# Retention scores by row halves, states by head with one scan, one mask table: a fused retention and Fourier-mixing kernel on one core

## The chip, the cores and the metric

The kernel runs on one core of a Trainium2 chip. The metric is the device time of one execution in microseconds (us). The kernel before takes 236.49 us, the median of three runs (236.26 to 236.76). The profile of before is one more execution, of 236.86 us.

The engines of a core work side by side, each through its own queue in program order: TensorE (PE in the profile; its weight loads are PEld), VectorE (DVE), ScalarE (ACT), GpSimd (POOL) and SyncE (SP), which issues transfers. Engines wait for each other by semaphores. TensorE writes only into PSUM, which has eight banks here used as a few shared slots; VectorE and ScalarE empty them.

## The reference

Inputs are q, k, v of shape (4 batches, 8 heads, 768 tokens, 64) and two weight matrices (512 x 2048 and 2048 x 512).

1. Retention: for each head a 64 x 64 state is carried along the tokens, `state = gamma[h] * state + k_t v_t^T` with `gamma[h] = 1 - 2^(-5-h)`, and `y_t = q_t state / 8`. The heads side by side give x of shape (4, 768, 512).
2. Fourier mixing: `u = x + real(FFT over tokens and features of x)`.
3. Layer norm of u without weights, then `out = u + relu(un @ w_ch1) @ w_ch2`.

## The kernel before

**Retention in chunks.** Tokens go in 6 chunks of 128 (`NCH = 6`). Heads go in four pairs per batch (`PAIR_ORDER`), 64 + 64 = 128 partitions. For each pair and chunk there are three products:

- *Scores* inside the chunk, keys by queries, masked and weighted by the decay: `a_piece` (line 691) on TensorE, `ma_piece` (705) on VectorE.
- *Key-value products* of chunks 0 to 4, 64 x 64 for each head, from which the *states* at the chunk borders come by a decayed running sum: `kv_piece` (717) and `s_piece` (731).
- *Output*: scores by v (`y_piece`, 753) plus queries by the state of the chunk before (`yx_piece`, 744), gathered in PSUM (`wkY`), then scaled into x by `x_piece`, mostly on ScalarE.

**Batch 0 and the later batches differ.** Batch 0 has units of its own:

- `am_unit` (line 574) takes the scores of a head as a product over 64 partitions only, head 0 in the upper and head 1 in the lower half of the rows, each into its own PSUM bank. `ae_unit` (583) multiplies by one 128 x 128 table `maskf` and the head's constant at the same time.
- `kv0_unit` (598) takes the 64 x 64 product of each head alone, head 0 into PSUM partitions 0 to 63 and head 1 into 64 to 127, with the five chunks as the innermost index: element (e, c) lies at `5*e + c`.
- `sc_unit` (607) makes all five states of a pair by one `tensor_tensor_scan` over 320 values, with the decay table `gk5` (zero at c = 0, so that each column begins anew).
- `yx_unit` (630) reads `s16[sl, :, c - 1]`, again by halves of the rows.

Batches 1 to 3 use full 128-row products instead. `qTz` holds the queries of each head with zeros in the other head's 64 rows, so that one product of the pair's keys with 2 x 128 columns of `qTz` gives both heads' scores: six products of 256 columns a pair, in three pieces of two chunks, one PSUM bank a piece. `ma_piece` multiplies 512 values a partition with `maskp`, a table with a mask for every head, which eight units `mp0` to `mp7` fill on various engines early on. `kv_piece` takes the full 128 x 128 product of the pair, of which only the two diagonal blocks are used, in two banks (chunks 0 to 2, and 3 and 4). `s_piece` copies the first state and makes the other four by a `scalar_tensor_tensor` each, on VectorE, into `s16[P, 5, 128]`. `yx_piece` reads 64 neighbouring values of it.

**The rest of a batch.** The Fourier mixing is done with cosine and sine tables after folding tokens and features by symmetry (`fold_s`, `fold_d`, `fold_e`, `s1_piece` at 840, `s2_piece` at 1024, `u_piece`). Then come layer norm, a first layer (`h3_piece`, 1267; relu in `r3_piece`, 1276), and a second layer by a seven-product scheme on half blocks (`hs_piece`, `m_piece` at 1329, `p3_piece` at 1374). The scheme needs sums of weights, `wsum_unit`; one of them, `ws1`, is laid over the memory of `gk5`, which is no longer used after batch 0.

**What sets the order.** `ORDER` is a written list of some 1,450 units for the whole kernel, and `pin()` chains every engine's instructions in just that order. `ENGINES` gives, unit by unit, the engine of a copy or scaling (A ScalarE, D VectorE, P GpSimd). Units are named by batch, kind, part and pair: `2a0_1` is the first score piece of batch 2, pair 1. `f512` is a filler, a 512-column product on dummy data, used in batch 0's stretch. Waits follow from tiles: the pool `ps_g` has 5 PSUM slots shared by scores, key-value products, `wkY`, transposes and the Fourier products; `ps_pm` has 3 for the two layers. Loads of batches 2 and 3 wait for the last score product of pair 1 of the batch before (`a_of`).

Of the kernel before, what the change touches and what calls it, by code (L numbers as in the profile page):

```python
# [36 lines left out]
q0:A q1:P q2:A q3:P k00:D k10:P k20:P k30:A v00:P v10:P v20:P v30:P v31:P eq0:D eq1:D eq2:A  # L37
eq3:A ek00:A ek10:A ek20:A ek30:A x00:A x01:D x10:A x11:D x20:A x21:A x30:A x31:A tn0:D tn1:A
tn2:D tn3:D tn4:A gk0:P gk1:A gk2:P gk3:A gc00a:D gc01a:D gc01b:D gc10a:A gc11a:A gc11b:A
ste0:A ste1:A xn0:P xn1:P cdh0:A cdh1:P nsp:P hid5:A fs0a:D fs0b:D fla:D flb:D fha:D fhb:D  # L40
fd0:D fd1:D gr0:D gr1:A gr2:A gr3:P nid0:D nid1:A hid:P v01:P eb0:D v11:P eb1:D v21:P eb2:A
eb3:A mp6:A mp5:A qn1:A mp1:P qn2:A un1:D h00:A te1:D mp2:P xl2:P qn3:A xl3:P mp0:D qn0:D h02:A
h12:A qn4:A h13:A xu2:D h03:A un2:A h11:A h01:A te2:A xl4:P xu4:P xu3:P xl0:D un3:A xu0:D h10:A
h20:D un4:A h21:A qn5:D xl5:P 1ck1_0:P te3:A h22:A 1cq_0:D 1ck0_0:D 1ek_0:D 1eq0_0:A 1eq1_0:A
xu5:P 1cv_0:P 1s0_0:A un5:A 1cq_1:A te4:D 1ck0_2:A 1ck0_1:P 1ck1_1:P mp7:P 1eq1_1:A 1eq0_1:A
1cv_1:P 1ek_1:A 1x1_0:A mp3:P 1x0_0:A h23:A 1cv_2:P 1ck1_2:A 1s0_1:D te5:A 1cq_3:P 1cq_2:A
1ck0_3:P 1s0_2:D 1cv_3:P 1ek_2:A mp4:P 1eq1_2:A 1ck1_3:P 1eq0_2:A 0r1_12:A 1eq1_3:A 1eq0_3:A
1x1_1:A 1x0_1:A 1s0_3:A 0r1_5:A 1ek_3:A 0r1_7:A 0r1_8:A 1x0_2:A 1x1_2:A 2cv_1:A 2cq1_1:A
# [12 lines left out]
1r2_4:A 1r2_3:A 2q1_2:A 1r2_5:A 2q0_2:A 1r2_2:A 3x1_1:A 1r2_7:A 3cq1_3:P 2q1_4:D 3cv_2:A
3x0_1:A 2q0_4:D 3cq1_2:D 3cq0_2:A 3ck0_2:P 2q0_5:A 2q1_5:A 2ux1_3:P 3x0_0:A 2ux1_4:P 3s0_3:A
2ux1_2:P 2ux0_3:P 2r0_1:A 3s0_2:A 2ux0_2:P 2ux0_4:P 2r0_2:A 2r0_5:A 2r0_7:A 2ux1_5:P 2r0_3:A
2r0_4:A 2r0_0:A 2ux0_5:D 2r0_6:A 3x1_0:A 3x0_2:A 3x1_2:D 3x1_3:A 2r1_5:A 2r1_6:A 3x0_3:A
2r1_1:A 2r1_3:A 2r1_2:A 2r1_4:A 2r1_0:A 2r1_7:A 3g00:A 3g11:A 3gr11:A 3g01:A 3g10:A 3q1_1:A
3gr10:A 3q0_1:D 3q0_0:D 3q1_0:A 3q1_2:D 3q0_2:D 3ux0_0:P 2r2_6:A 3ux1_0:P 2r2_2:A 2r2_7:A
3ux0_1:P 3ux1_2:P 2r2_0:A 3ux1_1:P 3gr00:P 2r2_1:A 3ux0_2:P 2r2_3:A 2r2_5:A 2r2_4:A 3gr01:D
3q1_3:A 3q0_3:D 3ux0_3:P 3q0_5:A 3ux1_3:P 3r0_3:A 3q0_4:A 3q1_5:D 3r0_6:A 3r0_7:A 3r0_4:A
3r0_5:D 3r0_1:A 3r0_0:D 3q1_4:D 3r0_2:A 3ux1_5:P 3ux0_5:P 3ux0_4:P 3r1_1:A 3ux1_4:P 3r1_5:A
3r1_4:A 3r1_0:D 3r1_2:A 3r1_6:D 3r1_3:A 3r1_7:D 3r2_2:D 3r2_3:A 3r2_6:A 3r2_4:A 3r2_1:A 3r2_0:A  # L70
3r2_7:D 3r2_5:A
# [3 lines left out]
lq0 nid0 lk0 par gk3 f512 q0 lv0 qtz10 lq1 ta0 v00 ta1 tn1 f512 f512 f512 f512 tb1 si1 k00 tk0 qz0  # L75
q1 mp2 lk1 lv1 lq2 qtz00 lk2 ab1 tq0 lq3 tn0 gk2 eq0 tb0 ta2 tn2 f512 ek00 am01 ab0 ae010 nid1 kb0
k10 co1 tb2 si2 hid5 ab2 co2 ae011 tq1 am00 ae001 si0 f512 f512 eb0 ta3 tk1 ek10 lk3 f512 tn3 eq1
tb3 lv2 ab3 v01 kv0 ae000 yi01 kb1 gk0 v11 sc0 si3 q2 mp6 f512 v10 f512 k20 gk1 nsp yi00 co0 eb1
am11 ae110 ae111 am10 ae101 ae100 tk2 ek20 tq2 yx0 eq2 x01 kv1 q3 f512 x00 f512 f512 w10 w11 sc1
am21 ae210 ae211 am20 mp3 ae201 yi10 k30 ae200 kb2 eb2 yi11 yx1 x11 f512 x10 fs0a fs0b tk3 ta4 tq3  # L80
v20 ek30 v21 kv2 sc2 tn4 tb4 w12 kb3 eq3 am30 yi20 ae301 mp7 ae300 ab4 am31 hid ae311 si4 eb3 yi21
yx2 ae310 stx01 lv3 v30 v31 kv3 s1s10 w13 w20 sc3 x20 x21 flb yi31 yi30 co4 fla fd1 yx3 f512 s1s00
x30 fd0 s1m1 x31 fha fhb co3 cdh0 xn0 g0a s1m0 xm0 gc00a s1s01 gc01a gc10a xmb xn1 s1s11 gc11b
gc11a w21 g0b g0c gc01b stx3 stg00 stx4 stg01 cdh1 xm2 stg10 stg11 stx2 ste1 half qe1 s22 qn2 gr0
ste0 close px1 s21 qn1 uu1 xm1 ul1 gr3 gr1 gr2 mu1 un1 h00 h03 ul2 w22 s20 xl2 uu2 qn0 s23 qn3 xu2
s25 xe qz1 ul3 qtz01 ut1 uu0 te1 xl3 ul0 h01 w23 h02 mu2 0p0_0 un2 bn2 mp0 xl0 s24 qn4 uu4 ul4 xl4
uu3 qn5 ul5 xl5 xu3 h11 pad11 ut2 te2 h13 1lq0 1lk0 h10 1lq1 xu0 bn0 1lk1 h22 bn1 bn3 xu4 1lv0 h20
h21 0rt0 bn4 0p1_0 uu5 0p2_0 un3 h12 1cq_1 0p3_0 xu5 0p0_2 1cq_0 1tq0 1tq1 1ck1_0 1ck1_1 1ck0_0
1tk0 1lq2 un4 ut4 bn5 0p1_2 1ek_0 1eq0_0 0rc0 mp1 0o0 0p0_1 1ck0_1 te4 1tk1 1eq1_0 1a2_0 qtz11
1a0_0 1m0_0 un5 1eq0_1 1eq1_1 1cq_2 1lk2 1cv_0 1m2_0 1ek_1 1lv1 1cv_1 pad01 1lk3 1ck0_3 1lq3 1cq_3  # L90
1kv0_0 1s0_0 0p1_1 1s1_0 ut3 te3 0p2_1 1a1_0 1kv1_0 1m1_0 1a0_1 1m0_1 1ck0_2 1a2_1 1s2_0 0p3_1
1s3_0 1s4_0 1lv3 1m2_1 1a1_1 1ck1_2 1tk2 1ek_2 ut5 te5 1m1_1 h23 1tq2 1kv0_1 1s0_1 1ck1_3 1cv_3
1yx_0 1y1_0 mp5 1y0_0 1eq0_2 1eq1_2 1s1_1 1s2_1 1kv1_1 1x1_0 1lv2 1cv_2 0o1 1x0_0 2lq1 2lk1 0p2_2
0p3_2 1s3_1 1a1_2 1s4_1 1m1_2 1tk3 1ek_3 1a0_2 1m0_2 1tq3 1kv0_3 0h1_8 1s0_3 1s1_3 0o2 0r1_8 1yx_1
1y1_1 1y0_1 1eq0_3 1s2_3 pad10 1kv0_2 1s0_2 2lv1 1s1_2 0h1_6 1eq1_3 1x0_1 2lk0 1x1_1 1s2_2 1a2_2
0h1_12 2cq1_1 1kv1_2 1m2_2 1a0_3 0r1_6 2lk2 0r1_12 mp4 1s3_2 0h1_11 0r1_11 1s4_2 1m0_3 1a2_3 1m2_3
1yx_2 1kv1_3 1y0_2 1s3_3 1y1_2 1a1_3 1m1_3 1s4_3 0rt1 1x1_2 1x0_2 1fs00 1fs01 0h1_1 1fd01 0r1_1
# [71 lines left out]
def kernel(  # L169
# [518 lines left out]
    def a_piece(b, i, part):  # L688
        def run():
# [6 lines left out]
            if part == 2:  # L696
                a_of[b, i] = mm
# [931 lines left out]
```

## Time and profile before

| what | value |
|---|---|
| median of three runs | 236.49 us (236.26 to 236.76) |
| the profiled execution | 236.86 us |
| its span in the trace | 234.9 us |
| TensorE busy | 228.9 us |
| VectorE busy | 203.4 us |
| ScalarE busy | 144.3 us |
| GpSimd busy | 91.3 us |
| granted TensorE clock | 1.00 |

The span runs from the first to the last instruction of the program. A group is written as line, engine, operation, output <- inputs, form, count. For a matmul the form begins with rows*columns of the array in use: 128*128 is the whole of it, 64*128 half of the rows, 128*64 half of the columns. The length of a matmul includes the way through the array, in which the next has already begun; the pace is told by the distance from start to start.

### The profile page before, as it was taken

The page shows a single profiled execution, that of the slowest core. Times are in us where ns is not written, and L with a number is a line of the kernel's source. Part 1 is how long each engine was busy: PE and PEld are TensorE (multiplying, and loading weights), DVE is VectorE, ACT ScalarE, POOL GpSimd, SP SyncE. Part 2 cuts the span into 40 slices and gives each one's busy share as a digit, 9 for nine tenths or more (in the row PEclk, how much of TensorE's full clock was granted, in tenths as well). Part 3 has the DMA queues.
Part 4 walks back from the last instruction along what each step waited for, and adds up shares of the span by engine and source line. Part 5 has one row for each costly group of instructions (what it writes and reads, how often), then busy time and mean ns, then how long its engine had stood idle before and what let it go on. Part 6 is the DMA issues. An engine that isn't in the chain of part 4 may idle for free.

```text
span 234.9 us, 6332 instructions
## 1 busy us (share of the span) xinstructions
PE 228.9 (97%) x2471; PEld 187.1 (80%) x2471; DVE 203.4 (87%) x527; ACT 144.3 (61%) x303; POOL 91.3 (39%) x144
## 2 busy tenths in 40 slices
PE   7999999999999999999999999999999999999994
PEld 2566888856776855889999989888898988888884
DVE  6599989966899999999999999999988698875494
ACT  7599786688998856671976493565644615241220
POOL 4789133452440378226315707404007161330302
PEclk9999999999999999999999999999999999999999
DMA  7999997999999999999969956632700224130034
GB/s 199 311 290 178 207 166 116 257 228 247 220 213 201 211 209 176 198 195 182 237 161 202 201 129 126 156 77 81 237 3 4 45 89 114 22 47 0 4 125 143
DMA packets 94253, 36.45 MB, mean 155 GB/s; under 512 B 83600, under 2 KB 91408, under 8 KB 94224
## 3 DMA queue, kind: packets, MB, share of 16 engines
q1 hardware_dynamic: 89856, 31.79, 63.9%
q0 software_dynamic: 4224, 4.19, 11.5%
q8 instruction: 19, 0.31, 0.6%
q14 instruction: 10, 0.08, 0.1%
q10 hardware_dynamic: 144, 0.07, 0.1%
HBM read 27.26 MB, written 6.29 MB: 143 GB/s over the span
## 4 chain that ended last, share of the span: by engine, by line
PE 73%; ACT 1%; DVE 0%; issue 0%
PE psh L1267 27%; PE psc L1329 24%; PE psc L1223 6%; PE psh L1183 4%; PE wkA L694 3%; PE ps L840 3%; PE pq L1024 2%; PE wkY L753 2%; PE wkY L744 1%; PE wkK L717 1%; ACT qTz L262 1%; PE tq L669 1%; PE psh L1205 0%; PE pst L1167 0%; PE ps L974 0%; ACT x L267 0%
## 5 line engine op out<-in xcount | busy, mean ns | idle before, releaser
L1267 PE MATMUL psh<-unT,w 128*128 128x256 f16 x576 | 67.7, 273 | 0.0
L1267 PEld LDWEIGHTS <-w 128*128 128x128 f16 x576 | 55.8, 98 | 6.6 <-DVE u L1374 0.2
L1276 ACT ACTIVATE ht<-psh 128x512 f16<-128x512 f32 x65 | 37.4, 596 | 30.5 <-PE psh L1267 22.7
L1329 PEld LDWEIGHTS <-ht 128*128 128x128 f16 x360 | 34.1, 98 | 4.2 <-DVE ht L1300 0.3
L1329 PE MATMUL psc<-w,ht 128*128 128x256 f16 x192 | 26.2, 272 | 0.0
L705 DVE TENSOR_TENSOR atm<-wkA,maskp 128x512 f16<-128x512 f32 x36 | 23.9, 682 | 1.5 <-PE wkA L694 1.5
L1060 POOL TENSOR_TENSOR u<-u,x 128x256 f32<-128x256 f32 x31 | 19.7, 654 | 14.2 <-DVE u L1050 7.9
L1223 PE MATMUL psc<-w,ht 128*128 128x512 f16 x96 | 23.3, 379 | 0.0
L1374 DVE TENSOR_TENSOR u<-psc,u 128x256 f32<-128x256 f32 x42 | 16.7, 416 | 6.6 <-PE psc L1329 5.8
L1374 POOL TENSOR_TENSOR u<-u,cd 128x512 f32<-128x512 f32 (+1 forms) x8 | 8.9, 1119 | 27.9 <-DVE cd L1374 27.9
L267 ACT ACTIVATE x<-wkY,gexp 128x384 f16<-128x384 f32 x29 | 16.1, 583 | 5.6 <-PE wkY L753 4.1
L731 DVE SCALAR_TENSOR_TENSOR s<-s,gk,wkK 128x128 f16<-128x128 f16 x48 | 16.1, 341 | 2.2 <-ACT s L262 1.5
L1118 DVE BATCH_NORM_STATS2 bst<-u 128x6 f32<-128x512 f32 x24 | 16.3, 681 | 0.2
L263 POOL COPY g16r<-g 128x384 f16<-128x384 f16 x6 | 3.4, 579 | 31.5 <-ACT g L262 19.0
L1223 PEld LDWEIGHTS <-ht 128*128 128x128 f16 x96 | 8.7, 98 | 7.7
L262 ACT COPY qn<-pq 128x127 f32<-128x127 f32 (+2 forms) x31 | 7.9, 299 | 11.0 <-PE pq L1024 5.1
L1374 POOL TENSOR_TENSOR u<-u,ws 128x256 f32<-128x256 f32 (+1 forms) x6 | 5.7, 978 | 20.5 <-DVE ws L1374 20.5
L1399 ACT ACTIVATE un<-u,stats 128x512 f16<-128x512 f32 x12 | 9.5, 812 | 5.8 <-DVE stats L1392 5.8
L694 PE MATMUL wkA<-qTz,kT 128*128 128x256 f16 x72 | 12.4, 272 | 0.3 <-ACT unT L262 0.2
L268 POOL TENSOR_SCALAR kd<-k,gexp 128x384 f16<-128x384 f32 x15 | 9.4, 629 | 6.8 <-DMA k<-in_k_dram 4.8
L1183 PE MATMUL psh<-unT,w 128*128 128x384 f16 x64 | 11.9, 326 | 0.0
L1205 PE MATMUL psh<-unT,w 128*128 128x128 f16 x192 | 11.7, 219 | 0.0
(238 smaller groups left out, 508.5 us busy)
## 6 DMA issues: line engine op xcount, KB each, us to landing
q<-in_q_dram SPq DMA_DIRECT2D x16, 384.0 KB, 6.2
k<-in_k_dram SPq DMA_DIRECT2D x16, 384.0 KB, 5.6
v<-in_v_dram SPq DMA_DIRECT2D x16, 384.0 KB, 6.3
w<-in_moe_w_ch_dram POOLq DMA_DIRECT2D x8, 512.0 KB, 7.8
out_dram<-u SPq DMA_DIRECT2D x6, 512.0 KB, 3.4
out_dram<-u SPq DMA_DIRECT2D x6, 256.0 KB, 3.9
out_dram<-o SPq DMA_DIRECT2D x2, 512.0 KB, 3.2
out_dram<-o SPq DMA_DIRECT2D x3, 128.0 KB, 1.8
```

The source lines that it names most:

```text
L267: return nc.scalar.activation(out, in_, AF.Copy, bias=0.0, scale=scale)
L694: mm = nc.tensor.matmul(wk[:, c2], st["kT"][:, c, :], st["qT"][:, :, c, :], start=True, stop=True)
L705: nc.vector.tensor_tensor(out=st["atm"][:, 2 * part:2 * part + 2], in0=st["wk", part], in1=maskp[:, PAIR_ORDER[i]].unsqueeze(1).to_broadca ...
L731: nc.vector.scalar_tensor_tensor(out=s16[:, c], in0=s16[:, c - 1], scalar=gk2[:, hp:hp + 1], in1=st["kv", c // 3][:, c % 3], op0=ALU.mult, ...
L1060: (nc.vector if on.get(f"{b}ux{n}_{kb}", "P") == "D" else nc.gpsimd).tensor_tensor(out=u[:, lo:hi], in0=u[:, lo:hi], in1=x[:, 1, 257:1:-1] ...
L1118: nc.vector.bn_stats(bst, lb[b]["u"][:, kb, :])
L1183: nc.tensor.matmul(psh, w116[:, cb, fb * P:(fb + 1) * P], lb[b]["unT"][:, cb, rt * 384:(rt + 1) * 384], start=(cb == 0), stop=(cb == 3))
L1223: nc.tensor.matmul(lb[b]["psc", rb], ht16[:, fb, rb % 3 * P:rb % 3 * P + P], w216[:, fb, :], start=(fb == 0), stop=(fb == NFB - 1))
L1267: nc.tensor.matmul(psh[:, t], w116[:, cb, fb * P:(fb + 1) * P], lb[b]["unT"][:, cb, p * 256:(p + 1) * 256], start=(cb == 0), stop=(cb == 3))
L1276: nc.scalar.activation(dst, psh, AF.Relu, bias=0.0, scale=1.0)
L1329: nc.tensor.matmul(o if c1 - c0 == 256 else o[:, c0:c1], lh(f), r, start=first and f == 0, stop=last and f == 7, skip_group_check=True)
L1374: (nc.vector if e == "D" else nc.gpsimd).tensor_tensor(out=o, in0=x, in1=y, op=ALU.add)
```

## The change

Batches 1 to 3 take batch 0's forms for three steps of the retention, and the written order and the engines of the units are new throughout:

- *Scores*: twelve products over 64 rows instead of six over 128, in two pieces of three chunks; each piece fills two banks, one a head. The mask step becomes four operations of 3 x 128 values a pair, with the one table `maskf` and the head's constant. `maskp` and its eight units go.
- *Key-value products and states*: `kv0_unit` and `sc_unit` now serve all batches, one bank and one scan a pair. `kv_piece` and `s_piece` go.
- *State products*: `yx_piece` stays at full height with `qTz`, but reads the state as `s16[:, :, c - 1]`, whose 64 values lie 5 apart.
- `ws1` becomes a tile of its own, since `gk5` is needed to the end.
- `ORDER` has 1,381 units instead of 1,450, with one `f512` less; many units of `ENGINES` change place or engine.

```diff
-    maskp = const.tile([P, NHP, 2, P], f32, tag="maskp")
+    ws1 = const.tile([P, 8, 256], f16, tag="ws1")
...
-    def kv0_unit(i):
+    def kv0_unit(i, b=0):
         def run():
-            st = st_of(0, i)
-            kd, v16 = kd_of[0, i], v16_of[0, i]
+            st = st_of(b, i)
+            kd, v16 = kd_of[b, i], v16_of[b, i]
...
-    def sc_unit(i):
+    def sc_unit(i, b=0):
...
     def a_piece(b, i, part):
         def run():
             st = st_of(b, i)
-            wk = st["wk", part] = ps_g.tile([P, 2, 2, P], f32, tag="g", name="wkA")
-            for c2 in range(2):
-                c = 2 * part + c2
-                mm = nc.tensor.matmul(wk[:, c2], st["kT"][:, c, :], st["qT"][:, :, c, :],
-                                      start=True, stop=True)
-            if part == 2:
+            wk = st["wk", part] = [ps_g.tile([P, 3, P], f32, tag="g", name="wkA",
+                                             padded_shape=[P, 4, P]) for _ in range(2)]
+            for c3 in range(3):
+                c = 3 * part + c3
+                for h2 in range(2):
+                    sl = slice(D * h2, D * h2 + D)
+                    mm = nc.tensor.matmul(wk[h2][:, c3, :], st["kT"][sl, c, :],
+                                          st["qT"][sl, h2, c, :], start=True, stop=True)
+            if part == 1:
                 a_of[b, i] = mm
...
-    def ma_piece(b, i, part):
+    def ma_piece(b, i, part, h2):
...
-            nc.vector.tensor_tensor(
-                out=st["atm"][:, 2 * part:2 * part + 2], in0=st["wk", part],
-                in1=maskp[:, PAIR_ORDER[i]].unsqueeze(1).to_broadcast([P, 2, 2, P]),
-                op=ALU.mult)
+            nc.vector.scalar_tensor_tensor(
+                out=st["atm"][:, 3 * part:3 * part + 3, h2, :], in0=st["wk", part][h2],
+                scalar=float(gam[2 * PAIR_ORDER[i] + h2] ** (-P)),
+                in1=maskf.unsqueeze(1).to_broadcast([P, 3, P]), op0=ALU.mult, op1=ALU.mult)
...
-    def kv_piece(b, i, g):
...
-    def s_piece(b, i, c):
...
                     nc.tensor.matmul(yk[h2][:, c, :], st["qT"][:, h2, c, :],
-                                     st["s16"][:, c - 1, 64 * h2:64 * h2 + 64],
+                                     st["s16"][:, :, c - 1],
                                      start=(c == 1), stop=False, skip_group_check=True)
...
-    ws1 = gk5.rearrange("p h e c -> p (h e c)").bitcast(f16)[:, 0:2048].rearrange(
-        "p (f m) -> p f m", m=256)
```

More of the change, by code (lines that the diff above doesn't have):

```diff
@@ L36 @@
 ENGINES = """
[L37 to L48, printed above, removed]
@@ L67 @@
[L67 to L71, printed above, removed]
+q0:A q1:P q2:A q3:D k00:D k10:P k20:P k30:P v00:P v10:A v20:P v30:P v31:P eq0:D eq1:D eq2:A
+eq3:A ek00:D ek10:A ek20:A ek30:A x00:A x01:A x10:A x11:A x20:A x21:A x30:A x31:A tn0:A tn1:A
@@ new lines @@
+2cq0_0:A 1q1_2:A 2ck0_3:P 1q0_2:A 1gr11:A 1gr10:D 1q1_3:A 1q0_3:A 2cv_0:P 1ux0_1:P 1q0_5:A
+1ux1_0:P 1ux0_0:P 2ck0_2:P 1q1_5:A 1ux1_1:D 2ck1_2:A 1ux0_2:P 1q1_4:A 1ux0_3:P 2ck1_3:P
+1ux1_3:P 1ux1_2:P 2cq0_2:A 2cq1_2:A 1ux0_5:P 2cq0_3:P 2x1_1:A 1te0:A 1q0_4:A 1te1:A 2cv_2:A
+1r0_7:A 1r0_2:A 1r0_0:A 1r0_3:A 2x0_1:A 1r0_6:A 1r0_5:A 1r0_1:A 1ux1_5:P 1ux0_4:D 1ux1_4:P
+1r0_4:A 1te2:A 2x0_0:A 3ck1_0:A 3cv_1:P 3cq1_1:A 2x1_0:A 1r1_2:A 3ck1_1:A 3cq0_1:P 3ck0_1:P
+1r1_5:A 2x0_3:A 2x1_3:A 1r1_1:A 2x0_2:A 2x1_2:A 1r1_4:A 1r1_6:A 1r1_0:A 1r1_3:A 1r1_7:A 3cv_0:P
@@ L72 @@
+3r2_6:A 3r2_4:A 3r2_1:D 3r2_0:D 3r2_7:A 3r2_5:A
 """
@@ L80 @@
[L80 to L85, printed above, removed]
@@ new lines @@
+lv1 v11 v00 lq2 am01 ae010 ae011 v01 kv0 tn1 tb1 ab1 ta3 f512 k10 tk1 si1 lk2 ek10 nsp f512 lq3
+tn3 q2 kb1 sc0 am11 ae111 ae110 lk3 tb3 ab3 q3 f512 f512 tq2 gk3 am10 si3 ae101 k20 tk2 lv2 co1
+k30 yi01 yi00 yx0 f512 v10 eb1 ae100 kv1 sc1 w10 w11 ek20 kb2 eq2 am20 ae200 eb2 x00 tk3 v20 x01
+ek30 yi10 yi11 lv3 ae201 yx1 x10 x11 am21 ae211 ae210 fs0b tq3 ta4 v21 tn4 tb4 kv2 sc2 eq3 kb3 ab4
+yi21 am30 ae301 f512 stx01 ae300 am31 ae310 si4 yi20 yx2 eb3 hid5 co0 v31 x20 v30 kv3 ae311 sc3
+fs0a x21 flb f512 co3 fla fd0 w12 cdh1 w13 fd1 f512 f512 f512 yi31 yi30 yx3 x30 x31 xm0 fha s1s10
@@ new lines @@
+qe1 s1s00 xn0 co4 fhb s1m0 xmb gc00a s1m1 gc10a xn1 s1s01 s1s11 cdh0 gc11b stx3 stg00 g0a g0b
+gc01a gc01b px1 w20 s21 gr1 gc11a w21 xm1 gr2 g0c gr3 gr0 qz0 stx4 stg01 stg10 stg11 qn1 stx2 ul1
+qz1 s22 qn2 ul2 mu1 ste1 ste0 uu1 un1 half s23 qn3 close h02 w22 xm2 uu2 xu2 ul3 h03 mu2 h00 ut1
+te1 s20 qn0 uu0 qtz01 xl2 h01 0p0_0 un2 uu3 s24 w23 xl3 qtz11 ul0 h13 1lq0 xu3 bn3 qn4 ut2 xl0 te2
+xu0 h11 1lq1 un3 bn2 s25 0p1_0 qn5 pad11 ul5 h10 xl5 h20 h12 uu5 h22 xu5 bn5 ul4 uu4 xu4 bn1 1lk0
+un5 h21 bn0 0rt0 1cq_1 xe 0p2_0 xl4 bn4 ut3 te3 un4 ut5 1lk1 0p3_0 1lv0 1ck1_0 1ck0_0 1cq_0 0p0_2
@@ L352, in gk_unit @@
             gk2[:, hp:hp + 1].unsqueeze(1).to_broadcast([P, D, NCH - 2]))
-    def maskp_piece(h):
-        return lambda: scaled(on.get(f"mp{h}", "A"), maskp[:, h // 2, h % 2], maskf,
-                              float(gam[h] ** (-P)))
     def half_tables():
@@ L600, in kv0_unit @@
         return run
-    def sc_unit(i):
+    def sc_unit(i, b=0):
         def run():
-            st = st_of(0, i)
-            st["s16"] = sp.tile([P, D, NCH - 1], f16, tag="s16", name="s16",
-                                padded_shape=[P, P, NCH - 1])
+            st = st_of(b, i)
+            st["s16"] = sp.tile([P, D, NCH - 1], f16, tag="s16", name="s16")
             nc.vector.tensor_tensor_scan(
@@ L704, in run @@
                 st["atm"] = ap_.tile([P, NCH, 2, P], f16, tag="atm", name="atm")
-            nc.vector.tensor_tensor(
-                out=st["atm"][:, 2 * part:2 * part + 2], in0=st["wk", part],
-                in1=maskp[:, PAIR_ORDER[i]].unsqueeze(1).to_broadcast([P, 2, 2, P]),
-                op=ALU.mult)
-        return run
-    def kv_piece(b, i, g):
-        def run():
-            st = st_of(b, i)
-            wk = st["kv", g] = ps_g.tile([P, 3, P], f32, tag="g", name="wkK",
-                                         padded_shape=[P, 4, P])
-            for c in ((0, 1, 2), (3, 4))[g]:
-                nc.tensor.matmul(wk[:, c - 3 * g, :], kd_of[b, i][:, c].rearrange("p a b -> p (a b)"),
-                                 v16_of[b, i][:, c].rearrange("p a b -> p (a b)"),
-                                 start=True, stop=True)
-        return run
-    def s_piece(b, i, c):
-        def run():
-            st = st_of(b, i)
-            if c == 0:
-                st["s16"] = sp.tile([P, NCH - 1, P], f16, tag="s16", name="s16")
-                copied(on.get(f"{b}s0_{i}", "A"), st["s16"][:, 0], st["kv", 0][:, 0])
-                return
-            hp = PAIR_ORDER[i]
-            s16 = st["s16"]
-            nc.vector.scalar_tensor_tensor(out=s16[:, c], in0=s16[:, c - 1],
-                                           scalar=gk2[:, hp:hp + 1],
-                                           in1=st["kv", c // 3][:, c % 3],
-                                           op0=ALU.mult, op1=ALU.add)
+            nc.vector.scalar_tensor_tensor(
+                out=st["atm"][:, 3 * part:3 * part + 3, h2, :], in0=st["wk", part][h2],
+                scalar=float(gam[2 * PAIR_ORDER[i] + h2] ** (-P)),
+                in1=maskf.unsqueeze(1).to_broadcast([P, 3, P]), op0=ALU.mult, op1=ALU.mult)
         return run
@@ L1485, in first_units @@
                 U.update({f"pad{j}{h}": pad_unit(j, h), f"qtz{j}{h}": qt_zeros(j, h)})
-        for h in range(H):
-            U[f"mp{h}"] = maskp_piece(h)
         for b in range(B):
@@ L1514, in later_units @@
                         add(**{f"d{'qk'[n]}{i}": dma_t_piece(b, i, n)})
-                for n in range(3):
-                    add(**{f"a{n}_{i}": a_piece(b, i, n), f"m{n}_{i}": ma_piece(b, i, n)})
                 for n in range(2):
-                    add(**{f"kv{n}_{i}": kv_piece(b, i, n), f"y{n}_{i}": y_piece(b, i, n),
+                    add(**{f"a{n}_{i}": a_piece(b, i, n)})
+                    add(**{f"m{n}{h2}_{i}": ma_piece(b, i, n, h2) for h2 in range(2)})
+                for n in range(2):
+                    add(**{f"y{n}_{i}": y_piece(b, i, n),
                            f"x{n}_{i}": x_piece(b, i, n)})
-                for c in range(NCH - 1):
-                    add(**{f"s{c}_{i}": s_piece(b, i, c)})
+                add(**{f"kv_{i}": kv0_unit(i, b), f"sc_{i}": sc_unit(i, b)})
                 add(**{f"yx_{i}": yx_piece(b, i)})
```

194 lines of the change are left out of this document (95 added, 99 removed).

## The prediction

> **What bounds the kernel now.** I read the page's engine shares first, then the busy table by stage, then the timeline of TensorE alone. The page says who is busiest:
>
> ```profile
> span 234.9 us, 6332 instructions
> PE 228.9 (97%) x2471; PEld 187.1 (80%) x2471; DVE 203.4 (87%) x527; ACT 144.3 (61%) x303; POOL 91.3 (39%) x144
> ...
> PE   7999999999999999999999999999999999999994
> ...
> PE 73%; ACT 1%; DVE 0%; issue 0%
> ```
>
> TensorE is busy 97% of the span, and the chain that ended last runs almost only through it. A 97% could still hide stages in which another engine sets the pace, so the second view gives each engine's busy time by stretch (start:end and length, then PE, PEld, DVE, ACT, POOL, granted clock, DMA share, GB/s):
>
> ```profile
> core 0: us, PE busy (x) PEld busy (x) DVE busy (x) ACT busy (x) POOL busy (x), PEclk, DMA share, GB/s
> 0.00:30.00 30.00, 28.27 (x320) 17.44 (x321) 24.41 (x72) 24.09 (x49) 19.21 (x42) 1.00 1.10 236
> 30.00:80.00 50.00, 48.96 (x597) 37.99 (x596) 43.31 (x121) 41.61 (x83) 16.67 (x27) 1.00 1.08 204
> 80.00:130.00 50.00, 50.00 (x516) 40.51 (x514) 48.08 (x114) 32.22 (x75) 23.43 (x36) 1.00 1.08 197
> 130.00:180.00 50.00, 50.00 (x552) 44.93 (x551) 47.37 (x119) 28.80 (x62) 17.46 (x23) 1.00 0.50 116
> 180.00:234.90 54.90, 51.66 (x494) 46.24 (x492) 40.19 (x105) 17.60 (x38) 14.58 (x19) 1.00 0.23 64
> ```
>
> Batches 1 to 3, the "later batches", do the changed work between 50 and 165 us, and there TensorE is busy 48.96 of 50, then 50.00 of 50 twice. VectorE is close behind (48.08 of 50) but does not hold TensorE up. So what the change does to TensorE's own time goes one to one into the span, and relief on other engines is worth at most the 1.04 us that TensorE is idle in the second row.
>
> "Busy" counts overlapping matmuls once and tells nothing of their pace. The pace is the distance between the starts of neighbouring groups, so I read the timeline of TensorE (start, length, line, operands, form, count). First the present forms of the later batches:
>
> ```profile
> 62.81 0.38 PE L694 MATMUL wkA<-qTz,kT 128*128 128x256 f16 x2
> 63.03 0.50 PE L669 MATMUL tq<-ident,kd 128*128 128x128 f16 x6
> ...
> 63.92 0.33 PE L717 MATMUL wkK<-v,kd 128*128 128x128 f16 x3
> 64.09 0.33 PE L1183 MATMUL psh<-unT,w 128*128 128x384 f16 x1
> ...
> 60.34 0.45 PE L744 MATMUL wkY<-s,qTz 128*128 128x64 f16 x10
> 60.62 0.51 PE L753 MATMUL wkY<-v,atm 128*128 128x64 f16 x12
> 60.98 0.28 PE L717 MATMUL wkK<-v,kd 128*128 128x128 f16 x2
> 61.09 0.38 PE L1223 MATMUL psc<-w,ht 128*128 128x512 f16 x1
> ```
>
> Two score matmuls take 63.03 - 62.81 = 0.22 us, so 0.109 each; five key-value products take 0.17 + 0.11 = 0.28; ten state products (L744) take 0.28, the twelve after them 0.36, so about 0.029 each for 64 columns. Nothing is lost at the borders.
>
> Batch 0 already uses the forms that the change brings: L574 is the score by row halves (64*128), L598 the key-value product by column halves (128*64), L630 a product that reads the state laid out by head. Its timeline:
>
> ```profile
> 15.27 0.34 PE L620 MATMUL wkY<-v,atm 128*128 128x64 f16 x6
> 15.54 0.51 PE L574 MATMUL wkA<-qTz,kT 64*128 64x128 f16 x12
> ...
> 17.05 0.53 PE L630 MATMUL wkY<-s,qTz 64*128 64x64 f16 x10
> 17.51 0.47 PE L598 MATMUL wkK<-v,kd 128*64 128x64 f16 x10
> 17.91 0.82 PE L258 MATMUL wps<-ht 128*128 128x512 f16 x3
> 18.67 0.51 PE L574 MATMUL wkA<-qTz,kT 64*128 64x128 f16 x12
> 19.11 0.35 PE L620 MATMUL wkY<-v,atm 128*128 128x64 f16 x6
> ...
> 19.63 0.34 PE L620 MATMUL wkY<-v,atm 128*128 128x64 f16 x6
> 19.90 0.53 PE L630 MATMUL wkY<-s,qTz 64*128 64x64 f16 x10
> ...
> 23.02 0.34 PE L574 MATMUL wkA<-qTz,kT 64*128 64x128 f16 x6
> 23.30 0.35 PE L620 MATMUL wkY<-v,atm 128*128 128x64 f16 x6
> ```
>
> Here the borders cost. Six L620 should take 6 x 0.029 = 0.175, but the next group, of halves, starts 0.27 later, both at 15.27 and at 19.63: **entering** a group of halves costs 0.095 us. Twelve L574 last 0.44 until a full group starts, six last 0.28: six more cost 0.16, so one costs 0.027 (two halves run beside each other in 0.055), and 0.28 - 0.16 = 0.12 is the price of **leaving**. TensorE seems to run nearly empty whenever the shape of the array changes.
>
> **The change part by part, in TensorE time.** There are 12 later pairs of heads.
>
> *Scores.* Removed: 6 x 0.109 = 0.65 us a pair. Added: two pieces of six halves, each 0.28 with its leaving and 0.095 for entering, so 0.75. The halves alone would take 12 x 0.027 = 0.33 and save 0.32; two entries and two exits take that back. +0.10 a pair, +1.2 us in all.
>
> *Key-value products.* Removed 0.28. Added: ten column halves, 17.91 - 17.51 = 0.40 with leaving, and 0.095 for entering: 0.495. The halves are no quicker inside (the two heads together need what one full product needed). +0.215 a pair, +2.6 us.
>
> *Fewer borders.* Alone, 24 score pieces and 12 products would make 72 changes of shape. In the instruction order of the two kernels I count 27 now and 94 then: 67 more, since some groups stand side by side. 5 x 0.1: -0.5 us.
>
> *State products (yx_piece).* Their count and full-array form stay, but the state they read is now laid out as batch 0's is: the 64 values of one chunk lie 5 halfwords apart instead of next to each other. No row shows a full-height product reading so. The nearest is L630: ten in 17.51 - 17.05 = 0.46, less 0.1 for leaving, is 0.36, 0.073 for each two halves. If the two streams run side by side, as the L574 halves do, each one takes 0.073, and so does a full-height product that reads the same 64 values: 10 x 0.073 - 0.28 = +0.45 a pair, +5.3 us. If the two halves took turns, it is 0.036 each: +0.08 a pair, +0.9 us. If the spacing costs nothing: 0. Below nothing there is no reason. I take +5.3, since the L574 halves do overlap and L630's 64 columns at L744's pace would need only 0.029.
>
> *Fillers.* One product on dummy data goes from the start (23 instead of 24): 18.67 - 17.91 for three, less 0.095, is 0.22 each. -0.2 us.
>
> *Other engines.* Rows of the groups kept apart by shape (busy, mean ns | idle before):
>
> ```profile
> L705 DVE TENSOR_TENSOR atm<-wkA,maskp 128x512 f16<-128x512 f32 x36 | 23.9, 682 | 1.5 <-PE wkA L694 1.5
> L583 DVE SCALAR_TENSOR_TENSOR atm<-wkA,maskf 128x384 f16<-128x384 f32 x16 | 7.9, 546 | 0.3 <-PE wkA L574 0.2
> L731 DVE SCALAR_TENSOR_TENSOR s<-s,gk,wkK 128x128 f16<-128x128 f16 x48 | 16.1, 341 | 2.2 <-ACT s L262 1.5
> L607 DVE TENSOR_TENSOR_SCAN s<-gk,wkK 128x320 f16<-128x320 f32 x4 | 3.3, 813 | 0.0
> ```
>
> VectorE loses 36 x 0.682 + 48 x 0.341 = 40.9 us and gains 48 x 0.546 + 12 x 0.813 = 36.0: 5 us lighter. Twelve state copies and eight mask pieces go from ScalarE, VectorE and GpSimd; the reassigned casts and copies fall mostly on ScalarE, which is idle 39% of the span. All of that lies beside a full TensorE: 0, and at most -1.1 by the idle time above. The own tile for the weight sums lifts a wait on batch 0's decay table, which is done long before: 0. SyncE issues the same transfers in another order. Batch 2's loads now stand close ahead of their casts, with some key transposes ahead of loads; a late load would hold a cast on ScalarE or GpSimd and the copies queued behind it, then TensorE. I cost it at 0, because a slower TensorE gives transfers more time; without that cover it is the third rival's price.
>
> **Sum**: 1.2 + 2.6 - 0.5 + 5.3 - 0.2 = +8.4 us on the profiled execution's 236.86 (span 234.9 and 2.0 around it), so 245.3. That execution lies 0.37 above the median of 236.49: **244.9 us** forecast.
>
> **The rivals.**
> 1. *Cheap spacing.* The state products cost 0 to +0.9 instead of +5.3: +3.1 to +4.0, 239.6 to 240.5. For it: L630 could be two streams taking turns. Against: L574's halves do not. The Trainium skill, "SBUF — State Buffer", section "Door 1: The DMA port swizzle", says that strided reads are free up to 8 bf16 values, by which 5 would be free and this rival right (240); the same note asks for two hits in each 16-byte line, which a step of 10 bytes gives only in part, and the trace's 0.073 against 0.029 speaks for that half of it.
> 2. *Faster.* Batch 0's borders and L630's pace are batch 0's own waits for operands (TensorE is idle 1.7 of the first 30 us) and don't come along to the later batches. Then scores save 0.32 x 12 = 3.9, the products cost nothing more, with the filler -4.1: 232.4. It decides once borders and spacing together cost under 0.32 us a pair; I have 0.42 for the scores' four borders alone. Against: the entry has the same 0.095 at 15.27 and 19.63, with different things on either side. The Trainium skill, "TensorEngine Tiling (Array Packing)", section "Theoretical Speedup", gives up to 2x for contractions of 64, which is this rival; the section "Key Properties" says that a change of tiling mode drains the engine, which is what the rows show.
> 3. *New waits.* A score piece now holds two of the five shared PSUM banks until two VectorE operations of 0.546 are through, and loads come closer to their casts. Price: 2 to 5 us of TensorE idle time on top, 247 to 250. Against: VectorE gets 5 us lighter.
>
> **How the numbers follow.** Forecast as summed (243 to 247) 0.52; cheap spacing 0.22; new waits 0.18; faster 0.06; gains and borders cancelling within 0.2% 0.02. About 0.2% (0.5 us) is what a measurement of this kernel can tell from no change. Faster 0.06, same 0.02, slower 0.92. The range 239.5 to 248.5 takes in the forecast, the cheap spacing and the lower half of the new waits; it leaves out some 0.17.
>
> **What would show it.** In the timeline after: six score halves between full groups take 0.28 and their entry 0.095; ten wkK halves 0.40; ten state products 0.73 (cheap spacing: 0.3 to 0.37). TensorE stays busy 49 to 50 of each 50 us until about 240; if new waits arise, this falls below 48. VectorE's busy time falls to about 198. The forecast is wrong if the borders overlap with loads of weights in the later batches, or if the full-height product reads spaced values at the pace of contiguous ones.

## The result and the profile after

The changed kernel takes 243.12 us in the median of four runs (242.37 to 243.55), beside 236.62 for the kernel before: a ratio of 1.0273, 95% interval 1.0245 to 1.0302. It is 6.5 us slower. Measured a second time, it gave 242.99 beside 236.21, ratio 1.0290 (1.0256 to 1.0324). The profiled execution took 243.55, against 236.86 before.

The page of after, its shares first:

```profile
span 241.8 us, 6535 instructions
PE 235.3 (97%) x2602; PEld 188.5 (78%) x2602; DVE 204.8 (85%) x500; ACT 145.3 (60%) x301; POOL 82.0 (34%) x129
...
PE 93%; DMA 2%; ACT 2%; DVE 1%; issue 1%; DVEq 0%; ACTq 0%
```

TensorE is still busy 97% of a span that is 6.9 us longer. The busy table by stretch (columns as before) shows whether it waits more or has more to do:

```profile
0.00:30.00 30.00, 27.47 (x324) 17.67 (x325) 24.95 (x73) 25.17 (x53) 17.41 (x38) 1.00 1.03 229
30.00:80.00 50.00, 50.00 (x635) 37.53 (x633) 42.46 (x108) 35.11 (x67) 17.50 (x27) 1.00 1.11 204
80.00:130.00 50.00, 50.00 (x537) 38.11 (x535) 46.23 (x104) 33.11 (x73) 16.58 (x26) 1.00 1.05 190
130.00:180.00 50.00, 49.76 (x553) 43.21 (x551) 45.10 (x101) 31.49 (x67) 13.89 (x19) 1.00 0.65 128
180.00:241.80 61.80, 58.06 (x565) 51.94 (x563) 46.05 (x119) 20.39 (x45) 16.67 (x21) 1.00 0.19 57
```

It has more to do: 50.00, 50.00 and 49.76 of 50 us. Where the time is, the timeline of TensorE shows. L686 is now `a_piece`, L588 `kv0_unit`, L710 `yx_piece`, L719 `y_piece`:

```profile
62.27 0.38 PE L1189 MATMUL psc<-w,ht 128*128 128x512 f16 x1
62.49 0.34 PE L719 MATMUL wkY<-v,atm 128*128 128x64 f16 x6
62.76 0.34 PE L686 MATMUL wkA<-qTz,kT 64*128 64x128 f16 x6
63.03 0.82 PE L1149 MATMUL psh<-unT,w 128*128 128x384 f16 x4
63.69 0.50 PE L658 MATMUL tq<-ident,kd 128*128 128x128 f16 x6
64.12 0.47 PE L588 MATMUL wkK<-v,kd 128*64 128x64 f16 x10
64.52 0.89 PE L710 MATMUL wkY<-s,qTz 128*128 128x64 f16 x10
65.24 0.36 PE L719 MATMUL wkY<-v,atm 128*128 128x64 f16 x6
...
97.08 0.49 PE L1231 MATMUL psh<-unT,w 128*128 128x256 f16 x3
97.50 0.34 PE L686 MATMUL wkA<-qTz,kT 64*128 64x128 f16 x6
97.77 0.61 PE L1231 MATMUL psh<-unT,w 128*128 128x256 f16 x4
```

Read it as the prediction reads batch 0. Six L719 should take 0.175, the halves start after 62.76 - 62.49 = 0.27: 0.095 for entering. Three L1231 should take 3 x 0.109 = 0.33, the halves start after 0.42: 0.09 again, in the middle of the feed-forward layers. A score piece lasts 0.27 until the next full group starts, ten key-value products 64.52 - 64.12 = 0.40, and ten state products 65.24 - 64.52 = 0.72 where they took 0.28.

Summing over the whole trace the distance from each matmul's start to the next one's, by function, gives the account of the 6.9 us:

| TensorE, start to start, us | before | after | change |
|---|---|---|---|
| state products of the later batches | 3.49 | 8.60 | +5.1 |
| score products, with their leaving | 8.59 | 6.47 | -2.1 |
| key-value products of the later batches, with leaving | 3.82 | 4.70 | +0.9 |
| entering 23 score groups and 11 key-value groups, 0.096 each | - | 3.3 | +3.3 |
| one filler less | 8.77 | 8.60 | -0.2 |

The key-value figure of after is 6.31 for the whole function less 4 x 0.40 for batch 0. The 0.096 of an entry is the median over the score groups; the key-value groups have 0.093. The sum is +7.0. What the table leaves out cancels: no other function, batch 0's among them, moves by more than 0.5 us either way once the entries are taken from it.

### The profile page after: what moved, and what is told of

It is laid out like the page before. It is cut to its first block, busy times and chain, and to the rows that moved or that the text cites. A ratio compares the mean times of both kernels' runs of the same rounds, so it can differ in the third digit from the quotient of the medians.

```text
span 241.8 us, 6535 instructions
## 1 busy us (share of the span) xinstructions
PE 235.3 (97%) x2602; PEld 188.5 (78%) x2602; DVE 204.8 (85%) x500; ACT 145.3 (60%) x301; POOL 82.0 (34%) x129
## 3 DMA queue, kind: packets, MB, share of 16 engines
q0 software_dynamic: 4224, 4.19, 10.9%
## 4 chain that ended last, share of the span: by engine, by line
PE 93%; DMA 2%; ACT 2%; DVE 1%; issue 1%; DVEq 0%; ACTq 0%
PE psh L1231 26%; PE psc L1293 21%; PE psc L1189 9%; PE psh L1171 4%; PE psh L1149 4%; PE wkY L710 4%; PE wps L252 3%; PE wkA L686 3%; PE wkK L588 2%; PE ps L806 2%; DMA qTz<-q16z 2%; PE wkY L719 2%; PE pq L990 2%; PE tq L521 1%; PE tq L658 1%; PE pq L1040 1%
## 5 line engine op out<-in xcount | busy, mean ns | idle before, releaser
L1231 PE MATMUL psh<-unT,w 128*128 128x256 f16 x576 | 67.4, 273 | 0.0
L1231 PEld LDWEIGHTS <-w 128*128 128x128 f16 x576 | 55.3, 98 | 7.0
L1293 PEld LDWEIGHTS <-ht 128*128 128x128 f16 x360 | 33.8, 98 | 5.0 <-issue 0.7
L1026 POOL TENSOR_TENSOR u<-u,x 128x256 f32<-128x256 f32 x30 | 19.0, 646 | 30.8 <-DVE u L1012 17.7
L697 DVE SCALAR_TENSOR_TENSOR atm<-wkA,maskf 128x384 f16<-128x384 f32 x48 | 25.1, 546 | 4.1 <-PE wkA L686 3.9
L261 ACT ACTIVATE x<-wkY,gexp 128x384 f16<-128x384 f32 x32 | 17.5, 584 | 4.3 <-PE wkY L719 3.5
L1293 PE MATMUL psc<-ws,ht 128*128 128x256 f16 x120 | 16.5, 273 | 0.0
L596 DVE TENSOR_TENSOR_SCAN s<-gk,wkK 128x320 f16<-128x320 f32 x16 | 13.0, 811 | 2.1 <-PE wkK L588 1.2
L1189 PEld LDWEIGHTS <-ht 128*128 128x128 f16 x96 | 8.5, 98 | 7.7
L1171 PEld LDWEIGHTS <-w 128*128 128x128 f16 x192 | 11.1, 98 | 0.4
L710 PE MATMUL wkY<-s,qTz 128*128 128x64 f16 x120 | 10.8, 251 | 0.0
L1293 PEld LDWEIGHTS <-hsum 128*128 128x128 f16 x112 | 9.8, 98 | 1.0
```

What stands on the lines that cost most here:

```text
L261: return nc.scalar.activation(out, in_, AF.Copy, bias=0.0, scale=scale)
L697: nc.vector.scalar_tensor_tensor(out=st["atm"][:, 3 * part:3 * part + 3, h2, :], in0=st["wk", part][h2], scalar=float(gam[2 * PAIR_ORDER[i ...
L710: nc.tensor.matmul(yk[h2][:, c, :], st["qT"][:, h2, c, :], st["s16"][:, :, c - 1], start=(c == 1), stop=False, skip_group_check=True)
L1026: (nc.vector if on.get(f"{b}ux{n}_{kb}", "P") == "D" else nc.gpsimd).tensor_tensor(out=u[:, lo:hi], in0=u[:, lo:hi], in1=x[:, 1, 257:1:-1] ...
L1171: mm = nc.tensor.matmul(psh[:, f], w116[:, cb, fb * P:(fb + 1) * P], unT[:, cb, kb * P:(kb + 1) * P], start=(cb == 0), stop=(cb == 3))
L1189: nc.tensor.matmul(lb[b]["psc", rb], ht16[:, fb, rb % 3 * P:rb % 3 * P + P], w216[:, fb, :], start=(fb == 0), stop=(fb == NFB - 1))
```

## The experiments

Two theories were set against each other. **Form**: the loss is TensorE's own time, from changes of array shape and from the spaced reading of the states. **Order**: the loss comes from the new written order and its waits. A third question was whether the row halves are worth anything. Times are set side by side only where the kernels ran together on one chip, with runs of the kernel before among them; otherwise the ratios to the kernel before are compared.

### Spaced states alone, in the old order

```diff
-                st["s16"] = sp.tile([P, NCH - 1, P], f16, tag="s16", name="s16")
+                st["s16"] = sp.tile([P, 1, P, 5], f16, tag="s16", name="s16")
...
-                                     st["s16"][:, c - 1, 64 * h2:64 * h2 + 64],
+                                     st["s16"][:, 0, 64 * h2:64 * h2 + 64, c - 1],
```

(`s_piece` writes and reads the same places.)

> The kernel before, in its own written order, with one edit: the states of the later batches are stored with 5 halfwords from one value of a chunk to the next, as the changed kernel has them; scores, key-value products and the count of all instructions stay. If the spaced read sets the pace of the state products (0.072 us each in the profile of after, 0.029 before), they take 12 x 10 x 0.043 = 5.1 us longer and the time is 236.6 + 5.1 = 241.7. If instead the new written order or its neighbours slow them there, the products stay at 0.029 here and the time stays at 236.6. VectorE's state steps may become longer through the spaced writes; that would show in the group of their line and not in TensorE's pace.

Measured: 242.92 beside 235.57, ratio 1.0288 (1.0242 to 1.0334), +7.4 us. The groups by shape in its profile (busy, mean ns):

```profile
L731 DVE SCALAR_TENSOR_TENSOR s<-s,gk,wkK 128x128 f16<-128x128 f16 x48 | 26.7, 572 | 2.8 <-ACT s L262 2.2
L745 PE MATMUL wkY<-s,qTz 128*128 128x64 f16 x120 | 10.9, 251 | 0.4 <-DVE atm L705 0.2 <-DVE s L731 0.2
```

With the order untouched, the state products go from 5.5 busy to 10.9, and from 3.49 to 8.92 us start to start: +5.4. The order is therefore not the cause of this part. The other 2 us I put down to the edit's side effect, which was not shown apart: VectorE's state steps grew from 341 to 572 ns, and what depends on them comes later. The changed kernel has no such steps, as its scan writes in sequence.

### The spacing taken out of the changed kernel

```diff
+                st["sc16"] = sp.tile([P, NCH - 1, D], f16, tag="sc16", name="sc16")
+                copied("P", st["sc16"], raw.rearrange("p e c -> p c e"))
...
-                                     st["s16"][:, :, c - 1],
+                                     st["sc16"][:, c - 1, :],
```

> The changed kernel with the spacing undone for the later batches: the scan still writes 5 apart, and GpSimd copies the 320 values of a pair to a second tile in which a chunk's 64 values are neighbours; the state products read that. If the spaced read costs 5.1 us, the time is 243.1 - 5.1 = 238.0, plus what the 12 copies delay (GpSimd is busy 34%, and 2 to 20 us of TensorE work lie between scan and use in the written order, so I expect 0 to 0.5). If the loss comes from the written order and its waits, it stays at 243 or rises.

Measured: 244.17 beside 235.57, ratio 1.0349 (1.0294 to 1.0405). A miss: it is no faster than the changed kernel (1.0273 and 1.0290). Yet the state products fell from 8.60 to 3.52 us. The timelines of GpSimd and of TensorE in one stretch tell why:

```profile
66.11 0.53 POOL L257 COPY sc<-s 128x320 f16<-128x320 f16 x1 [3.00 <-DVE s L596]
66.61 0.84 POOL L262 TENSOR_SCALAR q16z<-q 128x768 f16<-128x768 f32 x1
```
```profile
65.35 0.34 PE L722 MATMUL wkY<-v,atm 128*128 128x64 f16 x6
67.50 0.51 PE L661 MATMUL tq<-ident,q16z 128*128 128x128 f16 x6 [1.81 <-POOL q16z L262]
```

The copy stood behind its scan in the written order, so GpSimd waited 3.00 us for VectorE; the cast of the next queries stood behind the copy, and TensorE waited 1.81 us for that cast. In all TensorE was not busy for 11.1 us of the span, against 6.6 in after. And right behind this wait the granted clock was 0.50 for a while (columns of the table by stretch):

```profile
67.95:71.36 3.41, 3.41 (x24) 1.34 (x22) 1.18 (x3) 2.81 (x5) 1.43 (x3) 0.50 1.28 224
```

That stretch costs about 1.7 us, an estimate: half of 3.41. It did not come in every execution: two had a mean clock of 0.998 and took 243.29 us, two had 0.993 and 0.991 and took 245.06 and 245.18. So waits, and in part the clock behind them, had taken the place of the work removed. Then the copies were made units of their own, some on another engine:

```diff
+    def cp_unit(b, i):
+        def run():
+            st = st_of(b, i)
+            st["sc16"] = sp.tile([P, NCH - 1, D], f16, tag="sc16", name="sc16")
+            copied("D" if (b, i) in ((1, 2), (1, 3), (2, 2), (2, 3), (3, 2)) else "P",
+                   st["sc16"], st["s16"].rearrange("p e c -> p c e"))
+        return run
```

> The changed kernel with neighbouring states again, but with the copies as units of their own, so that no cast queues behind a copy that waits for its scan: seven on GpSimd, set about 1 to 2.5 us of TensorE work ahead of their use, five on VectorE right behind the scan. In the first try TensorE's state products fell from 8.60 to 3.52 us in all, but GpSimd's queue, held by the copies, gave TensorE new waits. If that reading holds, the time falls by 4 to 5 us against the changed kernel, to 238 to 239. If it stays within 1 us of the changed kernel, the spaced read was no cause of the end time in this order.

For the comparison the changed kernel itself ran beside it:

> The changed kernel once more, unaltered, to stand on the same chip as the next three: 243.1 as first measured, or about 1.027 times the kernel before on this chip.

Measured: 238.14 (ratio to before 1.0089, 1.0056 to 1.0122), and 242.99 for the changed kernel: -4.9 us, as expected. The timeline of the stretch that was shown of after:

```profile
62.92 0.47 PE L587 MATMUL wkK<-v,kd 128*64 128x64 f16 x10
63.32 0.46 PE L716 MATMUL wkY<-sc,qTz 128*128 128x64 f16 x10
63.62 0.34 PE L725 MATMUL wkY<-v,atm 128*128 128x64 f16 x6
```

Ten state products take 0.30 again, while the key-value products before them keep their 0.40. With the trace (5.1 us in the starts) and the time (4.9) in agreement, the spaced reading is shown to be worth some 5 of the 6.5 us.

### Steps of 4 and of 2

```diff
+                t = sp.tile([P, (NCH - 1) * P], f16, tag="s16", name="s16")
+                st["s16"] = [t[:, c // 4 * 4 * P:c // 4 * 4 * P + 4 * P].rearrange(
+                    "p (e c) -> p c e", c=4)[:, c % 4] for c in range(4)]
+                st["s16"].append(t[:, 4 * P:])
```

(The kernel before; with 2 in place of 4 for the second.)

> The kernel before with the states of chunks 0 to 3 stored 4 halfwords apart (8 bytes, two values in 16 bytes) and chunk 4 with neighbours. If a step of up to two values in 16 bytes is free, as the Trainium skill, SBUF — State Buffer, section on the DMA port swizzle, has it in its parenthesis, the spaced eight products stay at 0.029 us each and the time at 236. If every step from 1 costs in proportion, they take some 0.06 and the time is 240.

> The kernel before with the states of chunks 0 and 1, and of 2 and 3, interleaved at a step of 2 halfwords (four values in 16 bytes), chunk 4 with neighbours. A step of 4 took 0.060 us a product of 64 columns, a step of 5 took 0.073, neighbours 0.029. Per 16 bytes touched that is 0.060 / 32 and 0.073 / 40, both 0.0018 to 0.0019. If the number of 16-byte lines is what counts, a step of 2 touches 16 and needs 0.030, which 64 columns hide: 0.029 to 0.031 each and no loss. If the step itself counts, in proportion, it is 0.040.

Measured, one run each: 238.13 beside 236.21, and 235.69 beside 235.39. The pace is the result here. Step 4, then step 2:

```profile
63.28 0.70 PE L747 MATMUL wkY<-s,qTz 128*128 128x64 f16 x10
63.81 0.51 PE L756 MATMUL wkY<-v,atm 128*128 128x64 f16 x12
```
```profile
63.54 0.46 PE L747 MATMUL wkY<-s,qTz 128*128 128x64 f16 x10
63.84 0.51 PE L756 MATMUL wkY<-v,atm 128*128 128x64 f16 x12
```

Ten products, of which eight are spaced, take 0.53 at a step of 4 and 0.30 at 2. In single distances from start to start: 0.029 for neighbours, 0.030 at 2, 0.060 at 4, 0.073 at 5. Sixty-four values at these steps touch 8, 16, 32 and 40 pieces of 16 bytes, and the last two give 0.0018 to 0.0019 us a piece; at a step of 2 that is 0.030, which 64 columns cover. So the note that the first rival cited (the Trainium skill, "SBUF — State Buffer", section "Door 1: The DMA port swizzle") does not hold here in either half: two values in 16 bytes were not enough, and steps of 4 and 5 halfwords were not free. Four values in 16 bytes were. That the pieces of 16 bytes are what counts is not shown: a price of some 0.015 us for each halfword of the step, hidden up to a step of 2, fits the four points as well. A step of more than 8 would tell the two apart and was not run.

### Full-height scores in the changed kernel

```diff
-                    sl = slice(D * h2, D * h2 + D)
-                    mm = nc.tensor.matmul(wk[h2][:, c3, :], st["kT"][sl, c, :],
-                                          st["qT"][sl, h2, c, :], start=True, stop=True)
+                    mm = nc.tensor.matmul(wk[h2][:, c3, :], st["kT"][:, c, :],
+                                          st["qT"][:, h2, c, :], start=True, stop=True)
```

> The changed kernel with scores at full height: each of the twelve products of 128 columns runs over 128 rows (queries padded with zeros in the other head's rows) instead of 64, into the same banks, in the same order and number. No change of array shape is left at the scores. By the prices of the forecast a piece of six takes 6 x 0.056 = 0.336 instead of 0.28 + 0.095 = 0.375, so 24 pieces give back 0.9 us: 242.2. If changes of shape cost nothing and the halves simply overlap, the halves are worth 24 x (0.336 - 0.165) = 4.1 us and this kernel goes to 247.

Measured: 243.65, ratio 1.0337 (1.0288 to 1.0386). It can't be read against the changed kernel, which did not run beside it, and in its profiled execution the granted clock fell to 0.66 between 10 and 20 us. So it ran again beside it:

> The changed kernel with full-height scores again, beside the changed kernel itself, because the granted clock fell in the first 20 us of its profile before. Borders and pace: 0.7 to 0.9 us under the changed kernel. Halves that are worth their overlap: 4 us over it.

Measured: 242.49 (ratio to before 1.0264, 1.0227 to 1.0301) and 242.99 for the changed kernel. The difference of 0.5 lies inside the two intervals, but it is far from the +4 us that overlapping halves without borders would have lost. The timeline of the piece shown of after:

```profile
96.82 0.60 PE L1230 MATMUL psh<-unT,w 128*128 128x256 f16 x4
97.26 0.50 PE L685 MATMUL wkA<-qTz,kT 128*128 128x128 f16 x6
97.59 2.13 PE L1230 MATMUL psh<-unT,w 128*128 128x256 f16 x18
```

Four L1230 take 0.44, so nothing is lost on entering, and six full products 0.33. With halves it was 0.27 and 0.095. Six halves with their two borders and six full products of twice the height cost nearly the same, 0.365 and 0.33; over 24 pieces that is some 0.8 us at most, of which the times show 0.5 and can't tell it from nothing. The row halves are thus worth nothing here in pieces of six.

### All parts, in the old order

> All parts of the change (scores by row halves, key-value products by column halves with one scan, spaced states, one mask table, own tile for the weight sums) in the written order and with the engines of the kernel before; the third score piece, the second key-value piece and the single state steps fall out of the list, the rest keeps its place. If the form of the products is the cause, TensorE needs as long as in after, and the time is 243 to 245 (before's order had some 1 us of waits at the removed groups). If the new order is the cause, it is near 237.

The edit is the diff of the change without its `ENGINES` and `ORDER`. In the old list the two score pieces stand at the first two of the three old places, each with its mask steps, and units that no longer exist were struck.

Measured: 246.09 beside 235.57, ratio 1.0425 (1.0380 to 1.0470). The state products take 8.59 us start to start, as in after. The time is 1 us above the expected range: TensorE was not busy for 9.9 us of the span, against 6.6 in after. The new order is not the cause of the loss: by the ratios, the same parts are some 3 us slower without it.

### Halves alone in the old order, apart and joined

> The kernel before with one part of the change: scores by row halves in two pieces of three chunks and four mask operations a pair with the one table, at the places of the first two of the three old pieces; key-value products, states and their layout stay, and the unused mask tables are still filled. In the instruction order some pieces stand together, so 38 changes of array shape come in, not 48. Halves 12 x 0.33 = 4.0 us, borders 38 x 0.095 = 3.6, against 7.85 for the full products: -0.3, so 235.9 beside 236.2, plus waits where a mask step is not ready. If borders cost nothing: 232.3.

> The same, with the two score pieces of a pair back to back (mask steps behind them where they stood too early): 24 changes of shape instead of 38, four of the five shared PSUM banks taken at once. By the price of a border it gains 14 x 0.095 = 1.3 us on the unjoined one, to 234.6, if the banks bring no waits; if borders cost nothing, it is no better than the unjoined one, or worse by the waits.

```diff
-1a2_0 ... 1a0_0 1m0_0 ... 1m2_0 ... 1a1_0 ... 1m1_0
+1a0_0 ... 1a1_0 1m00_0 1m01_0 ... 1m10_0 1m11_0
```

(The written order of one pair in the first of the two kernels, as an example; functions as in the change.)

Measured: 248.53 and 250.32 beside 235.39, ratios 1.0539 (1.0486 to 1.0592) and 1.0631 (1.0556 to 1.0707). Both missed by over 12 us. What TensorE waited for in the first, then in the second:

```profile
PE wkA L696 <- DVE atm L707: 2.9, 2, 2.3
PE wkK L719 <- DVE atm L707: 2.0, 1, 2.0
...
PE wkA L696 <- ACT qTz L261: 1.0, 1, 1.0
PE wkA L696 <- DVE u L1048: 0.9, 1, 0.9
```
```profile
PE wkA L696 <- DMA kT<-kd: 3.0, 1, 3.0
PE wkA L696 <- DVE atm L707: 2.7, 5, 0.6
PE wkK L719 <- DVE atm L707: 2.0, 1, 2.0
PE wkY L746 <- DVE atm L707: 1.4, 2, 1.1
```

TensorE now waits for mask steps (`atm`), and once in the second for keys that a transfer brings (`kT`). In the first, the score groups took 14.45 us start to start, against 6.47 in the changed kernel, and TensorE was not busy for 14.1 us of the span, against 6.0 before. The granted clock fell as well. In the first kernel two waits, of 1.98 and 2.34 us, had such a stretch behind them:

```profile
97.41:100.82 3.41, 3.41 (x19) 2.42 (x17) 3.38 (x7) 1.30 (x2) 1.42 (x2) 0.50 0.83 131
158.85:162.26 3.41, 3.41 (x18) 2.44 (x17) 1.20 (x4) 1.58 (x4) 0.00 (x0) 0.50 0.05 10
```

By the estimate above that is another 3.4 us, and the mean clock of all four executions was 0.983 to 0.985. No rule follows: in the second kernel a wait of 1.98 us had a stretch at 0.50 behind it and the longest, 2.95 us, had none.

This is the third rival, new waits, in the place where it does occur: in an order that was not written for pieces of two banks. That the banks are what is short was not tried apart. Why the whole change in this order (246.09) is quicker than the halves alone was not tried either; its trace has fewer waits, and the granted clock stayed at 1.00. The price of a border can't be told from the times of this pair; in both traces the entry is again 0.096 in the median.

### Both mends together

> The changed kernel with both edits that helped it: full-height scores (242.5 beside 243.0) and neighbouring states by placed copies (238.1). If they add up: 237.6, still over the kernel before by the twelve key-value products by column halves with their borders, 1.8 to 2.6 us, less what the new order saves in waits.

Measured: 238.20 beside 235.39, ratio 1.0111 (1.0061 to 1.0162). Against 1.0089 with neighbouring states alone, the full-height scores add nothing that these runs can tell. With the spacing and the score borders gone, 1.1% (2.6 us) remain. The key-value products, still in column halves, account for +0.9 and 11 x 0.095, 1.9 us in TensorE's starts; that part was read from the trace and not undone by itself, and the rest was not traced. No version here beats the kernel before.

## Why the prediction was right

The forecast was 244.9 and slower; 243.12 came, 1.8 less. Step by step:

- **TensorE is the bound.** Right: it stays full, and the span grew by 6.9 us where its starts grew by 7.0.
- **State products, +5.3.** Right: +5.1 in after, +5.4 alone in the old order, -4.9 when undone. The choice between the ends, 0.073 each by the side-by-side reading of L630 or 0.036 by turns, was the decisive one, and the first rival (239.6 to 240.5) fell by it.
- **Borders.** Right in kind and price: 0.095 for entering and 0.27 for a piece of six showed in the later batches too, so the faster rival, that these gaps were batch 0's own waits, fell. Its count of 67 more changes of shape holds as well.
- **Scores, +1.2; key-value products, +2.6; fewer borders, -0.5.** Too high together: +3.3 forecast, +0.1 and +1.9 measured with their entries. The new groups cost what was forecast. What was off is the price of the old ones, which the prediction took at their pace alone ("Nothing is lost at the borders"): 72 old score products took 8.59 us start to start where 72 x 0.109 is 7.85, and 60 key-value products 3.82 instead of 3.35. Nearly all of these 1.2 us are four delays, of 0.39, 0.33, 0.28 and 0.14 us at 55.9, 56.6, 67.3 and 100.5 us, the first three of them waits for ScalarE; they are gone with the old groups and their order. The prediction had bounded such relief at 1.1 us and put it at 0.
- **New waits.** Right that the new order has none to speak of. What the prediction did not see is how much that order is worth: the same parts in the old one cost some 3 us more by the ratios.
- **Other engines at 0.** Right for the end time, wrong in a detail: VectorE was to fall to about 198 us busy and stands at 204.8. The four changed groups are 5 us lighter by their instructions, but other steps came to VectorE: all its instructions together fell only from 232.7 to 231.6 us, and they overlapped less.

## What to carry to other kernels

Where TensorE is full, read the pace from start to start, not the busy time, and price each change of array shape: here about 0.2 us for going in and out, which ate all that six products by row halves saved (6 x 0.028). In batch 0 a group of twelve halves took 0.44 + 0.095, against 0.65 for the six full products that it replaces, so longer groups could pay; the one order tried with such groups lost more to waits. Before a layout is changed for the engine that writes it, ask how the matmul will read it; the scan saved VectorE 6.6 us and its layout cost TensorE 5. And an edit that adds a step to an in-order queue can move the wait to whatever stands behind it.

## What the runs showed of the hardware

- The moving operand of a matmul has a price by its step: 64 halfword values took 0.029 us at a step of 1, 0.030 at 2, 0.060 at 4, 0.073 at 5.
- VectorE pays for the step as well. The state step, one `scalar_tensor_tensor` of 128 values, took 341 ns in the mean with neighbours, 353 at a step of 2, 458 at 4 and 572 at 5. At 4 the mean mixes two forms, and they show that the write is what costs: the 36 steps that write spaced values took 498 ns, the 12 that read spaced values and write neighbours 340.
- A 64 x 64 product for each of two column halves took 0.056 us for both, no less than one full product of 128 columns (0.056). Whether the reason is the spaced write into PSUM, the column halves or their weight loads (137 ns in the median, 98 for a full one) was not tried.
- Of the five waits of TensorE of 1.8 us or more in these traces, four had a stretch of 3.41 us at a granted clock of 0.50 behind them, and the longest (2.95 us) had none.
- The two profiles of the changed kernel differed by 0.8 us in span (241.8 and 241.0), nearly all of it in batch 0's transposes, tables and fillers; the later products agreed within 0.2 us in each function.
